# Attention decode on one Trainium2 core: moving the stationary block of the score matmuls 8b columns to the left

## Chip, cores, metric

One core of one Trainium2 chip. The metric is the device time of one execution in microseconds (us); less is better. Times are medians of several executions. Verdicts are "faster", "same" or "slower" with a threshold of 2%, or "unclear" when the interval holds the threshold. PE is the engine of the matmuls, PEld stands for its weight loads, DVE and ACT are the vector and the scalar engine, and SP is the engine whose queue issues the loads of the ring.

## The reference

A decoder block for one new token in each of four sequences: attention over the last 2048 cached keys, then a gated feed-forward layer. Cut to what matters:

```python
# B = 4 batches, D = 1024, Hq = 32 query heads, Hkv = 4 key heads, Dh = 128, W = 2048, F = 3584
q = (layernorm(x) @ wq).reshape(B, 1, Hq, Dh).transpose(0, 2, 1, 3)
k = repeat(k_cache[:, :, -W:, :], 8, axis=1)
v = repeat(v_cache[:, :, -W:, :], 8, axis=1)
p = softmax(einsum("bhqd,bhkd->bhqk", q, k) * Dh ** -0.5)
o = einsum("bhqk,bhkd->bhqd", p, v)
h = x + o.reshape(B, 1, Hq * Dh) @ wo
l = layernorm(h)
out = h + (silu(l @ w1) * (l @ w3)) @ w2
```

Each key head g serves eight query heads, and the four batches have separate softmaxes: 4 batches x 4 key heads x 8 queries are 128 rows of scores.

## The kernel before

Everything that comes from HBM goes through one ring of 160 KiB per partition. The loads are issued from one queue, in this order; a load is issued as soon as the last reader of the ring space that it overwrites is done.

```python
plan = [
    ("wq", load_rows, (0, wq_v, N_Q, 0, 4)),
    ("wq", load_rows, (32 * KIB, wq_v, N_Q, 4, 4)),
    ("k", load_kv, (64 * KIB, A_k_cache, 0)),      # keys of batches 0, 1
    ("k", load_kv, (96 * KIB, A_k_cache, 2)),      # keys of batches 2, 3
    ("v", load_kv, (128 * KIB, A_v_cache, 0)),     # values of batches 0, 1
    ("v", load_kv, (0, A_v_cache, 2)),             # values of batches 2, 3
    ("wo", load_rows, (32 * KIB, wo_v, D, 0, 32)),
    ("w1", load_rows, (96 * KIB, w1_v, N_F, 0, 8)),
    ("w3", load_rows, (0, w3_v, N_F, 0, 4)),
    # ... (w3's other half, w2 in four pieces)
]
```

w1 overwrites the keys of batches 2 and 3 and most of the values of batches 0 and 1. So it waits for the output matmuls of batches 0 and 1, which come after all scores and the softmax.

The queries are copied into a zeroed tile `qz`. Batch b has a region of 136 columns: for each key head g a block of 32, whose first 8 columns hold the queries, and 8 spare columns at the end.

```python
qz = act.tile([P, B, Hkv * QD + REP], BF16)        # QD = 32, REP = 8
nc.vector.memset(qz[:], 0.0)
# ... q matmuls, scaling, transposes
nc.vector.tensor_copy(
    out=qz[:, :, : Hkv * QD].rearrange("p b (g z) -> p b g z", g=Hkv)[:, :, :, :REP],
    in_=qt_ps[:].rearrange("p r (g x) -> p x g r", g=Hkv)[:, :B, :, :],
)
qz_v = qz[:].rearrange("p b y -> p (b y)")
# ...
def emit_scores(u):                                 # unit u: batch b, 512 keys n
    b, n = units[u]
    kT_v = kT_tiles[u][:].rearrange("d j (pp g) -> d g j pp", g=Hkv)
    for g in range(Hkv):
        z0 = (b * Hkv + g) * QD
        nc.tensor.matmul(
            scores_ps[QD * g : QD * (g + 1), n * 512 : (n + 1) * 512],
            lhsT=qz[:, b, g * QD : (g + 1) * QD],
            rhs=kT_v[:, g, :, :],
            start=(b == 0),
            stop=(b == B - 1),
        )

for u, (b, n) in enumerate(units):
    # ... 16 transposes of keys on PE, evicted to kT half by DVE, half by ScalarE
    if u >= 1:
        emit_scores(u - 1)
# ... row maximum, exponential over all 128 rows, transposes of the probabilities
for b in range(B):
    for j in range(JK):
        nc.tensor.matmul(OT_ps[:, b, :], lhsT=loaded["v"][b][:, j, :], ...)
    if b % BS == BS - 1:
        load_next()
```

In this kernel a column of a stationary block (128x32) becomes one of the 32 rows of scores that its matmul writes. In this version the queries of every batch stand in columns 0 to 7 of their block, so `start` and `stop` add the four batches' scores up in the same eight rows of each group, and the other 24 rows hold zeros.

## Time and profile before

| | before |
|---|---|
| time, median of 3 runs | 138.38 us (138.34 to 138.45) |
| profiled run | 138.12 us, span 136.3 us |
| bytes through the queue of the ring loads | 55.58 MB, 95.3% of sixteen engines' span |
| busy PE / DVE / ACT | 50% / 31% / 23% |
| score stage, start of first to start of last matmul | 29.6 to 54.9 us |
| w1 issued | 73.22 us |

The page of the kernel before: span, busy time of each engine, the granted TensorE clock in tenths over 40 slices, the DMA queue (packets, megabytes, share), and the chain that ended last, by engine and by line.

```profile
span 136.3 us, 2302 instructions
...
PE 67.9 (50%) x1035; PEld 42.9 (31%) x1035; DVE 42.6 (31%) x73; ACT 31.0 (23%) x36; POOL 1.7 (1%) x8
...
PEclk9999999999999999965555865897557777555577
...
q1 hardware_dynamic: 2592, 55.58, 95.3%
...
DMA 58%; PE 21%; ACT 13%; DVE 5%; issue 1%; SPq 0%; ACTq 0%
DMA ring<-in_B_w_dram 42%; DMA ring<-in_A_wq_dram 16%; PE kt_ps L263 9%; ACT kT L269 6%; PE scores_ps L248 5%; ACT z L304 3%; PE q_ps L215 2%; PE g_ps L403 2%; DVE rmax L280 2%; ACT Pm L285 2%; PE OT_ps L326 2%; DVE pT L294 1%; DVE z L300 1%; ACT L285 1%; DVE q_sb L225 1%
```

The DMA queue is busy 95.3% of the span, while no engine is busy much over half of it: the kernel is a stream of 55.58 MB with the arithmetic beside it. But the chain also lists PE, ACT and DVE with 39% together, and names the score matmuls with 5%. A chain lists what was last at each step.

The instructions of the query tile: count, shortest/median/longest in ns, first and last start in us.

```profile
L248 PEld LDWEIGHTS <-qz x64: 92/92/93, 29.4 to 54.9; 128*32 128x32 bf16 x64
L248 PE MATMUL scores_ps<-kT,qz x64: 608/609/612, 29.6 to 54.9; 128*32 128x512 bf16 x64
```

The 64 weight loads read blocks at four different offsets (272 bytes from batch to batch) and differ by 1 ns.

The PE timeline of the stretch before the scores (start us, us taken, what, and in brackets the idle time before it), and then the ring's queue around 73 us:

```profile
22.55 3.15 PE L215 MATMUL q_ps<-ring,xnT 128*4 128x512 bf16 x32 [5.92 <-DMA ring<-in_A_wq_dram]
...
27.45 2.03 PE L263 MATMUL kt_ps<-ident,ring 128*128 128x128 bf16 x33
29.62 0.62 PE L248 MATMUL scores_ps<-kT,qz 128*32 128x512 bf16 x4 [0.15 <-ACT kT L269]
```

```profile
73.22 0.33 SPq L93 DMA_DIRECT2D ring<-in_B_w_dram  x1
```

Stretches of the span. The last three columns are granted clock, mean share of the DMA engines, and GB/s.

```profile
core 0: us, PE busy (x) PEld busy (x) DVE busy (x) ACT busy (x) POOL busy (x), PEclk, DMA share, GB/s
15.00:30.00 15.00, 7.89 (x93) 3.82 (x85) 2.36 (x4) 2.04 (x3) 0.00 (x0) 1.00 0.97 416
30.00:45.00 15.00, 13.46 (x179) 9.17 (x175) 5.70 (x9) 8.39 (x9) 0.00 (x0) 1.00 1.01 428
45.00:57.00 12.00, 9.13 (x112) 5.47 (x109) 5.41 (x7) 5.97 (x6) 0.00 (x0) 1.00 1.00 427
76.00:84.00 8.00, 3.56 (x92) 2.97 (x96) 1.32 (x3) 0.00 (x0) 0.00 (x0) 0.71 0.94 403
84.00:90.00 6.00, 5.05 (x104) 3.92 (x96) 1.35 (x5) 0.00 (x0) 0.00 (x0) 0.79 0.98 423
```

From 15 to 57 us, where the scores are made, the DMA engines are at 0.97 to 1.01. They don't run short while PE works. (The view puts a packet's whole bytes and time down to the stretch in which it starts, which is how a share comes out over 1.)

### The profile page before, as it was taken

What the parts mean: (1) busy time and instruction counts of PE and PEld (TensorE: products, weight loads), DVE (VectorE), ACT (ScalarE), POOL (GpSimd) and SP (SyncE); (2) the same over time, 40 slices, a digit from 0 to 9 for tenths busy, and PEclk for the clock granted to TensorE, in tenths of its full rate; (3) what the DMA queues carried; (4) which work ended last, traced back from release to release, by engine and by line L of the source; (5) the groups of instructions that cost most, each with busy time, mean ns of one, the idle gap of its engine ahead of it and who ended that gap; (6) DMA issues with size and microseconds to landing.
All of it is one profiled execution on the core that took longest, in us unless ns stands there. A gap on an engine that the chain in (4) does not pass through costs nothing.

```text
span 136.3 us, 2302 instructions
## 1 busy us (share of the span) xinstructions
PE 67.9 (50%) x1035; PEld 42.9 (31%) x1035; DVE 42.6 (31%) x73; ACT 31.0 (23%) x36; POOL 1.7 (1%) x8
## 2 busy tenths in 40 slices
PE   0101803698989889105259538830096440900960
PEld 0100201274656565001149427610043210300840
DVE  6440000244444444609940030160000695070000
ACT  0400000155555646092944000000003300000001
POOL 5000000000000000000000000000000000000000
PEclk9999999999999999965555865897557777555577
DMA  5999899999999999997988989989799999989960
GB/s 156 462 462 443 385 413 418 423 447 423 428 437 409 437 437 423 435 582 341 538 385 365 524 365 442 459 353 522 328 412 463 434 437 447 429 388 409 426 261 5
DMA packets 2662, 55.75 MB, mean 409 GB/s; under 512 B 312, under 2 KB 344, under 8 KB 604
## 3 DMA queue, kind: packets, MB, share of 16 engines
q1 hardware_dynamic: 2592, 55.58, 95.3%
q8 instruction: 8, 0.13, 0.3%
q10 hardware_dynamic: 60, 0.02, 0.1%
q14 instruction: 2, 0.02, 0.0%
HBM read 55.59 MB, written 0.01 MB: 408 GB/s over the span
## 4 chain that ended last, share of the span: by engine, by line
DMA 58%; PE 21%; ACT 13%; DVE 5%; issue 1%; SPq 0%; ACTq 0%
DMA ring<-in_B_w_dram 42%; DMA ring<-in_A_wq_dram 16%; PE kt_ps L263 9%; ACT kT L269 6%; PE scores_ps L248 5%; ACT z L304 3%; PE q_ps L215 2%; PE g_ps L403 2%; DVE rmax L280 2%; ACT Pm L285 2%; PE OT_ps L326 2%; DVE pT L294 1%; DVE z L300 1%; ACT L285 1%; DVE q_sb L225 1%
## 5 line engine op out<-in xcount | busy, mean ns | idle before, releaser
L269 ACT COPY kT<-kt_ps 128x1024 bf16<-128x1024 bf16 x16 | 15.8, 1014 | 12.0 <-PE kt_ps L263 12.0
L263 PE MATMUL kt_ps<-ident,ring 128*128 128x128 bf16 x256 | 16.4, 219 | 0.0
L263 PEld LDWEIGHTS <-ring 128*128 128x128 bf16 x256 | 14.3, 98 | 5.0 <-issue 4.9
L267 DVE COPY kT<-kt_ps 128x1024 bf16<-128x1024 bf16 x16 | 11.1, 691 | 15.2 <-PE kt_ps L263 15.2
L215 PE MATMUL q_ps<-ring,xnT 128*4 128x512 bf16 x64 | 6.7, 596 | 12.0 <-DMA ring<-in_A_wq_dram 12.0
L403 PEld LDWEIGHTS <-hnT 128*32 128x32 bf16 x128 | 5.3, 137 | 23.1 <-issue 20.5
L248 PE MATMUL scores_ps<-kT,qz 128*32 128x512 bf16 x64 | 9.9, 609 | 3.1 <-ACT kT L269 3.1
L326 PE MATMUL OT_ps<-z,ring 128*128 128x32 bf16 x256 | 7.4, 185 | 6.7 <-ACT z L304 5.0
L403 PE MATMUL u_ps<-ring,hnT 128*32 128x448 bf16 x64 | 6.3, 572 | 8.3 <-DMA ring<-in_B_w_dram 8.3
L403 PE MATMUL g_ps<-ring,hnT 128*32 128x448 bf16 x64 | 5.4, 525 | 9.0 <-DMA ring<-in_B_w_dram 9.0
L433 PE MATMUL y_ps<-ring,hgT 128*32 128x256 bf16 x112 | 5.7, 370 | 8.4 <-DMA ring<-in_B_w_dram 8.3
L326 PEld LDWEIGHTS <-ring 128*128 128x128 bf16 x256 | 7.3, 103 | 7.4 <-issue 7.4
L433 PEld LDWEIGHTS <-hgT 128*32 128x32 bf16 x112 | 4.4, 129 | 10.3 <-issue 6.1
L215 PEld LDWEIGHTS <-xnT 128*4 128x4 bf16 x64 | 2.1, 116 | 16.2 <-issue 15.9
L353 PE MATMUL y_ps<-ring,o 128*32 128x256 bf16 x128 | 5.8, 365 | 2.0 <-DMA ring<-in_A_wo_dram 2.0
L443 ACT CAST res<-y_ps 128x256 bf16<-128x256 f32 x1 | 0.4, 372 | 26.5 <-PE y_ps L433 26.5
L304 ACT ACTIVATE z<-pt_ps,mask 128x512 bf16<-128x512 f32 x8 | 5.3, 687 | 3.5 <-DVE z L300 3.5
L225 DVE TENSOR_SCALAR q_sb<-q_ps 128x512 bf16<-128x512 f32 x1 | 0.7, 690 | 17.2 <-PE q_ps L215 17.2
L353 PEld LDWEIGHTS <-o 128*32 128x32 bf16 x128 | 4.8, 130 | 3.8 <-issue 3.1
L300 DVE TENSOR_SCALAR z<-pt_ps,mask 128x512 bf16<-128x512 f32 x8 | 5.5, 740 | 1.2 <-ACT z L304 0.8
L296 PE MATMUL pt_ps<-pT,perm 128*128 128x512 bf16 x4 | 2.4, 607 | 6.8 <-DVE pT L294 6.8
L417 DVE RECIPROCAL eg<-eg 128x896 f32<-128x896 f32 x1 | 5.8, 5753 | 0.0
(73 smaller groups left out, 40.5 us busy)
## 6 DMA issues: line engine op xcount, KB each, us to landing
ring<-in_A_wq_dram SPq DMA_DIRECT2D x2, 4096.0 KB, 16.8
ring<-in_A_k_cache_dram SPq DMA_DIRECT2D x4, 2048.0 KB, 25.5
ring<-in_A_v_cache_dram SPq DMA_DIRECT2D x4, 2048.0 KB, 40.2
ring<-in_B_w_dram SPq DMA_DIRECT2D x1, 7168.0 KB
ring<-in_B_w_dram SPq DMA_DIRECT2D x2, 3584.0 KB, 28.6
ring<-in_B_w_dram SPq DMA_DIRECT2D x1, 4352.0 KB
ring<-in_B_w_dram SPq DMA_DIRECT2D x1, 1792.0 KB
ring<-in_B_w_dram SPq DMA_DIRECT2D x1, 768.0 KB
```

The source lines that it names most:

```text
L215: nc.tensor.matmul(q_ps[QD * g : QD * g + B, hf * 512 : (hf + 1) * 512], lhsT=xnT[:, kc, :], rhs=wq_t[:, c0 : c0 + 512], start=(kc == 0), ...
L248: nc.tensor.matmul(scores_ps[QD * g : QD * (g + 1), n * 512 : (n + 1) * 512], lhsT=qz[:, b, g * QD : (g + 1) * QD], rhs=kT_v[:, g, :, :], ...
L263: nc.tensor.transpose(out=kt_ps[:, jj, :], in_=k_v[:, n * NJ + t * TB + jj, :], identity=ident[:])
L267: nc.vector.tensor_copy(out=kT[:, t * TB : (t + 1) * TB, :], in_=kt_ps[:])
L269: nc.scalar.copy(out=kT[:, t * TB : (t + 1) * TB, :], in_=kt_ps[:])
L300: nc.vector.tensor_scalar(out=z[:, :, g, :], in0=pt_ps[:], scalar1=mask[:, g : g + 1], scalar2=None, op0=ALU.mult)
L304: nc.scalar.mul(out=z[:, :, g, :], in_=pt_ps[:], mul=mask[:, g : g + 1])
L326: nc.tensor.matmul(OT_ps[:, b, :], lhsT=loaded["v"][b][:, j, :], rhs=PTz[j // NJ][:, (j % NJ) * B + b, :, :], start=(j == 0), stop=(j == J ...
L353: nc.tensor.matmul(y_ps[QD * j : QD * (j + 1), :], lhsT=o4[:, i, :, :].rearrange("p b s -> p (b s)"), rhs=loaded["wo"][i][:, j * CG : (j + ...
L403: nc.tensor.matmul(out_ps[QD * j : QD * (j + 1), hf, :HF], lhsT=hnT[:, k, :], rhs=loaded[kind][k][:, c0 : c0 + HF], start=(k == 0), stop=( ...
L417: nc.vector.reciprocal(out=eg[:], in_=eg[:])
L433: nc.tensor.matmul(y2_ps[QD * j : QD * (j + 1), :], lhsT=hgT[:, i, :], rhs=loaded["w2"][i][:, j * CG : (j + 1) * CG], start=False, stop=(i ...
```

## The change

The tile has the 8 spare columns so that a window of 32 columns can slide: started 8b columns further left, it holds batch b's queries in its columns 8b to 8b+7 and zeros elsewhere. The four batches then accumulate into rows of their own.

```diff
             nc.tensor.matmul(
                 scores_ps[QD * g : QD * (g + 1), n * 512 : (n + 1) * 512],
-                lhsT=qz[:, b, g * QD : (g + 1) * QD],
+                lhsT=qz_v[:, z0 : z0 + QD],
                 rhs=kT_v[:, g, :, :],
```

(b * 136 + 32g - 8b is b * 128 + 32g, which is z0.) The compiled instruction streams of the two kernels list the same operations, shapes and waits on all engines. One operand address differs.

Both versions pass the comparison with the reference, though only the later one computes it. A float32 calculation with the reference's formulas explains this: the scores have a standard deviation of 0.0025, so every softmax is nearly uniform. With batch 0's scores replaced by the sum over the batches and those of batches 1 to 3 by zero, as the earlier kernel's rows have it, the output moves by at most 8e-7, with a standard deviation of 0.05 of the output. These inputs can't tell right scores from wrong ones.

## The prediction

> **What bounds the kernel now.** HBM traffic. The page's DMA queue table gives 55.58 MB through the weight-and-cache queue at 95.3% of the sixteen engines' span. PE, DVE and ACT are busy 50%, 31% and 23%. The chain of waits is 58% DMA. PE (21%) and ACT (13%) enter it mostly from 27 to 55 us, where it alternates between key transposes, the ScalarE copy of kT (1.02 us) and four score matmuls (0.62 us). DMA is not short of work there: its share from 15 to 57 us is 0.97 to 1.01 (stretch table). The next load that this stage can hold back, w1, is issued at 73.2 us, when the second batch's output matmuls have freed its ring space; the previous load, wo, is still in flight then. Estimate: the loads up to wo are 33.6 MB, at about 428 GB/s (stretch table) 78 us, plus the 2 us start, so they end near 80 us. The score stage therefore has an estimated 5 to 7 us of slack.
>
> **What the change does.** It alters one operand address. The stationary block of the 64 score matmuls (16 units x 4 groups) has 128 x 32 bf16 in both versions, and only its first column moves, by 8b. Rows of scores: before, batch b's eight queries occupy columns 0 to 7 of each 32-column block for every b, and start/stop accumulate all four batches into the same rows. After, they are columns 8b to 8b+7; the other 24 are zeros of the same tile. So this repairs the meaning (four separate softmaxes); nothing is removed or added. The comparison of compiled instruction streams shows all five engines the same, 2063 PE rows in both, with the same waits.
>
> **Costs, from the trace.** 64 weight loads of 92 ns (min 92, max 93; 2.4 us) and 64 matmuls of 609 ns (608 to 612), four groups overlapping in 0.62 us. [...] Alignment: before, the blocks start at multiples of 272 bytes per batch, after at multiples of 256, yet before's 64 loads, over four different offsets, already differ by 1 ns at most. Net on this stage: 0.0 us, at most 0.1. Downstream, max (2.29 us), exponential (1.97 us) and the rest keep their shapes; only values change.
>
> [...] The granted clock before is 1.00 throughout the score stage and 0.50 to 0.73 later, where PE idles often.
>
> **On the critical path:** nothing. Even 5% of all score matmuls (0.5 us of 9.9) would disappear in the slack.
>
> **Prediction:** 138.4 us, range 137.9 to 138.9 (before: 138.34 to 138.45, its profiled run 138.12). Faster by over 2%: 1%; within 2%: 98%; slower by over 2%: 1%.
>
> **Signs that it is right:** 64 score weight loads of 92 ns and matmuls of 609 ns; last score matmul near 55 us; w1 issued near 73 us; 95% DMA share; PE clock 1.0 until 57 us. **Signs that it is wrong:** score weight loads over 100 ns, or w1 issued after 80 us with a dip in the DMA row behind it.
>
> **What would make it wrong:** a different chip or HBM state; a weight load that is dearer when its block straddles two batches' regions; an operand-dependent clock drop in the softmax or output stage large enough to push w1's issue past wo's end.

The sum came to 138.4 us, the time before plus 0.0 us (at most 0.1) for the change, with 5 to 7 us of slack (about 80 us for the end of wo, less 73.2 us for w1's issue). That the addresses would cost nothing was the estimate from the 1 ns by which the 64 loads of the trace differ; that the values would cost nothing was not shown by the trace. e4 and e3 test them. The 2 us start is read from the trace (the first packets of wq start at 1.74 us). PE was busy 88% of the score stage and 44% of the time from 57 to 136 us; the clocks of 0.50 to 0.73 are means of stretches of 8 to 16 us there.

## The result

| | before | after |
|---|---|---|
| time, median | 138.36 us (138.17 to 138.45, 4 runs) | 138.22 us (138.14 to 138.38, 4 runs) |
| ratio | | 0.9996, 95% interval 0.9981 to 1.0011 |
| score stage, first to last matmul | 29.6 to 54.9 us | 31.6 to 56.9 us |
| w1 issued | 73.22 us | 75.27 us |

Ratios are the mean time of one kernel's runs over that of the other's of the same rounds, so not quite the ratio of the medians quoted.

The page of the kernel after, the same lines:

```profile
span 136.5 us, 2302 instructions
...
PE 69.7 (51%) x1035; PEld 44.0 (32%) x1035; DVE 42.6 (31%) x73; ACT 31.1 (23%) x36; POOL 1.7 (1%) x8
...
PEclk9999999999999999965555555896558655555586
...
q1 hardware_dynamic: 2592, 55.58, 95.1%
...
DMA 56%; PE 24%; ACT 11%; DVE 5%; issue 1%; SPq 0%; ACTq 0%
DMA ring<-in_B_w_dram 40%; DMA ring<-in_A_wq_dram 16%; PE kt_ps L263 11%; ACT kT L269 5%; PE scores_ps L248 5%; ACT z L304 3%; PE q_ps L215 3%; PE g_ps L403 2%; DVE rmax L280 2%; ACT Pm L285 2%; PE OT_ps L326 1%; DVE pT L294 1%; DVE z L300 1%; ACT L285 1%; PE qt_ps L229 1%
```

The instructions of the query tile in the kernel after:

```profile
L248 PEld LDWEIGHTS <-qz x64: 92/92/102, 31.6 to 56.9; 128*32 128x32 bf16 x64
L248 PE MATMUL scores_ps<-kT,qz x64: 608/609/630, 31.6 to 56.9; 128*32 128x512 bf16 x64
```

Medians of 92 and 609 ns, as before; the longest are a little longer. The stage takes the same 25.3 us from first to last start. Yet it begins 2.0 us later, and w1 is issued 2.05 us later. The PE timeline and the ring's queue of the kernel after show from where on:

```profile
22.57 3.58 PE L215 MATMUL q_ps<-ring,xnT 128*4 128x512 bf16 x32 [6.10 <-DMA ring<-in_A_wq_dram]
...
27.98 3.73 PE L263 MATMUL kt_ps<-ident,ring 128*128 128x128 bf16 x33
31.64 0.64 PE L248 MATMUL scores_ps<-kT,qz 128*32 128x512 bf16 x4
```

```profile
75.27 0.33 SPq L93 DMA_DIRECT2D ring<-in_B_w_dram  x1
```

The second batch of q matmuls took 3.58 us where it had taken 3.15, and the first 33 key transposes 3.73 us where they had taken 2.03. Both precede the first score matmul, so the changed operand had not been used once. The later transposes take 1.07 us for 16 in both traces. It isn't later data either: PE's wait for wq ended at 22.55 and 22.57 us. And the stretches of the kernel after:

```profile
core 0: us, PE busy (x) PEld busy (x) DVE busy (x) ACT busy (x) POOL busy (x), PEclk, DMA share, GB/s
15.00:30.00 15.00, 8.08 (x75) 4.08 (x68) 1.68 (x3) 0.66 (x2) 0.00 (x0) 1.00 0.97 416
30.00:45.00 15.00, 13.65 (x172) 9.41 (x170) 5.54 (x8) 8.34 (x9) 0.00 (x0) 1.00 1.01 428
45.00:57.00 12.00, 10.42 (x136) 6.74 (x133) 4.84 (x7) 7.50 (x8) 0.00 (x0) 1.00 1.01 429
76.00:84.00 8.00, 4.79 (x153) 4.12 (x153) 1.33 (x3) 0.00 (x0) 0.00 (x0) 0.50 0.92 395
84.00:90.00 6.00, 5.11 (x118) 3.75 (x110) 1.34 (x5) 0.00 (x0) 0.00 (x0) 0.80 1.03 442
```

The DMA share is as before, and the total doesn't show the 2 us. The trace shows where they fade: the matmuls with wo start at 82.25 us before and 83.16 us after, because before they waited 2.04 us for wo to land, and after only 0.81 us for the eviction ahead of them. The first gate matmul starts at 99.06 us before and 98.96 us after, in both when w1 has landed.

So two things were left to show: that the lag has nothing to do with the change, and how much lag the stream of loads really absorbs. The latest issue of w1 that costs nothing is called the knee below; from the prediction's estimate of wo's end I first put it at 79.7 us.

### The profile page after: what moved, and what is told of

The parts are those of the page before. It is cut to its first block, busy times and chain, and to the rows that moved or that the text cites. A ratio compares the mean times of both kernels' runs of the same rounds, so it can differ in the third digit from the quotient of the medians.

```text
span 136.5 us, 2302 instructions
## 1 busy us (share of the span) xinstructions
PE 69.7 (51%) x1035; PEld 44.0 (32%) x1035; DVE 42.6 (31%) x73; ACT 31.1 (23%) x36; POOL 1.7 (1%) x8
## 3 DMA queue, kind: packets, MB, share of 16 engines
q1 hardware_dynamic: 2592, 55.58, 95.1%
## 4 chain that ended last, share of the span: by engine, by line
DMA 56%; PE 24%; ACT 11%; DVE 5%; issue 1%; SPq 0%; ACTq 0%
DMA ring<-in_B_w_dram 40%; DMA ring<-in_A_wq_dram 16%; PE kt_ps L263 11%; ACT kT L269 5%; PE scores_ps L248 5%; ACT z L304 3%; PE q_ps L215 3%; PE g_ps L403 2%; DVE rmax L280 2%; ACT Pm L285 2%; PE OT_ps L326 1%; DVE pT L294 1%; DVE z L300 1%; ACT L285 1%; PE qt_ps L229 1%
## 5 line engine op out<-in xcount | busy, mean ns | idle before, releaser
L263 PE MATMUL kt_ps<-ident,ring 128*128 128x128 bf16 x256 | 18.1, 232 | 0.0
L263 PEld LDWEIGHTS <-ring 128*128 128x128 bf16 x256 | 16.0, 105 | 4.9 <-issue 4.9
L215 PE MATMUL q_ps<-ring,xnT 128*4 128x512 bf16 x64 | 7.2, 626 | 12.0 <-DMA ring<-in_A_wq_dram 12.0
L326 PEld LDWEIGHTS <-ring 128*128 128x128 bf16 x256 | 7.4, 105 | 7.4 <-issue 7.4
L353 PE MATMUL y_ps<-ring,o 128*32 128x256 bf16 x128 | 5.2, 343 | 0.8 <-DVE o L342 0.8
L226 ACT ACTIVATE q_sb<-q_ps 128x512 bf16<-128x512 f32 x1 | 0.6, 597 | 21.4 <-DVE q_sb L225 21.4
```

The lines of the kernel that those rows point to most:

```text
L215: nc.tensor.matmul(q_ps[QD * g : QD * g + B, hf * 512 : (hf + 1) * 512], lhsT=xnT[:, kc, :], rhs=wq_t[:, c0 : c0 + 512], start=(kc == 0), ...
L263: nc.tensor.transpose(out=kt_ps[:, jj, :], in_=k_v[:, n * NJ + t * TB + jj, :], identity=ident[:])
L353: nc.tensor.matmul(y_ps[QD * j : QD * (j + 1), :], lhsT=o4[:, i, :, :].rearrange("p b s -> p (b s)"), rhs=loaded["wo"][i][:, j * CG : (j + ...
```

## The experiments

My theory: the changed address costs nothing at all. The 2.0 us belong to the execution and not to the change. (What I took for their cause was a guess that no run shows; it is cut from the expectations of e1 and e12.) They, and any other lag of the score stage, vanish as long as w1 is issued before the load ahead of it runs out. Rivals: the lag comes from the change; the data in the block change the clock; a weight load pays for its start address; the score stage is on the critical path, as the chain lists it, and something else made up for it.

### e1: the kernel before, once more

No edit.

> The kernel before, unedited, timed against itself: it measures the noise and gives a second trace of the same program. My theory (the 2.0 us by which the kernel after reached its first score matmul later, 31.6 against 29.6 us, is [...] not the change): ratio 1.000 with an interval of about 0.2%; the first score matmul anywhere from 29.5 to 31.7 us, a late one would settle it. Rival (the lag comes from the change): 29.6 us within 0.2 us, as in the first trace of before.

138.16 us (138.12 to 138.28, 5 runs), ratio 0.9996 (0.9984 to 1.0009). The PE timeline of this run:

```profile
22.62 3.58 PE L215 MATMUL q_ps<-ring,xnT 128*4 128x512 bf16 x32 [5.92 <-DMA ring<-in_A_wq_dram]
...
28.03 3.73 PE L263 MATMUL kt_ps<-ident,ring 128*128 128x128 bf16 x33
31.69 0.64 PE L248 MATMUL scores_ps<-kT,qz 128*32 128x512 bf16 x4
```

The unchanged kernel started its scores at 31.7 us here, with the same 3.58 and 3.73 us ahead of it, and issued w1 at 75.31 us. The rival is refuted: the lag belongs to the execution, not to the change.

### e2: the kernel after, once more

No edit.

> The kernel after, unedited, five rounds. My theory: ratio to before 0.998 to 1.002; score weight loads 92 ns and score matmuls 609 ns in the median; the first score matmul anywhere from 29.5 to 31.7 us. Rival (the lag comes from the change): first score matmul again at 31.6 us within 0.2 us. Rival (the shifted operand costs something): ratio above 1.002.

138.17 us (137.96 to 138.23, 5 runs), ratio 0.9994 (0.9981 to 1.0006); medians 92 and 609 ns (93 and 609 in e1); first score matmul at 31.6 us. The last number alone is what the rival expected as well; only e1, e3 and e4 tell them apart. The kernel before timed against itself (0.9996) and the kernel after (0.9994) can't be distinguished.

### e3: non-zero data in the idle columns

```diff
-    nc.vector.memset(qz[:], 0.0)
+    nc.vector.memset(qz[:], 0.05)
```

> After, with the query tile filled with 0.05 in place of 0.0 before the queries are copied in, so the 24 idle columns of each stationary block hold non-zero data (the scores are wrong on purpose). My theory: nothing depends on the values; ratio 0.998 to 1.002, weight loads 92 ns, matmuls 609 ns, granted clock 1.00 up to 57 us. Rival (operand data move the clock): a granted clock below 1.00 in the score stage, or matmuls over 620 ns in the median, and the stage from first to last score matmul longer than the 25.3 us of both first traces by over 1 us.

138.15 us (138.10 to 138.33, 4 runs), ratio 0.9997 (0.9983 to 1.0011); granted clock 1.00 from 30 to 57 us, where the stage lies. The query tile's instructions in this run:

```profile
L248 PEld LDWEIGHTS <-qz x64: 92/92/93, 29.8 to 55.3; 128*32 128x32 bf16 x64
L248 PE MATMUL scores_ps<-kT,qz x64: 608/609/611, 30.0 to 55.3; 128*32 128x512 bf16 x64
```

25.3 us from first to last start again. Neither the time nor the durations depend on these data. And with the changed address of the kernel after, the first score came at 30.0 us: an early start isn't tied to the kernel before either.

### e4: blocks that start at odd places

```diff
-                lhsT=qz_v[:, z0 : z0 + QD],
+                lhsT=qz_v[:, z0 + 3 : z0 + 3 + QD],
```

> After, with every stationary block starting three columns (6 bytes) further right, so that no block starts at a multiple of 16 bytes and blocks straddle neighbouring regions (scores are wrong on purpose). My theory: start address is free; weight loads 92 ns, matmuls 609 ns, ratio 0.998 to 1.002. Rival (a weight load pays for its start address): weight loads above 95 ns in the median; if by 10%, 9 ns times 64 is 0.6 us of load time, hidden in the total.

138.34 us (138.05 to 138.44, 4 runs), ratio 1.0001 (0.9984 to 1.0018). The query tile's instructions in this run:

```profile
L248 PEld LDWEIGHTS <-qz x64: 92/93/95, 29.5 to 55.0; 128*32 128x32 bf16 x64
L248 PE MATMUL scores_ps<-kT,qz x64: 608/609/612, 29.7 to 55.0; 128*32 128x512 bf16 x64
```

One ns more in the median than in before; but e1, the kernel before unedited, has 93 ns too. The start address is free within what this trace resolves. (First score at 29.7 us.)

### e5, e6, e7: a longer score stage

After each group of four score matmuls of a unit, the same four with an all-zero stationary block, X times; the result stays correct.

```diff
+    zz = act.tile([P, QD], BF16)
+    nc.vector.memset(zz[:], 0.0)
 ...
-        for g in range(Hkv):
+        X = 1 if b < 2 else 0              # e5;  e6: X = 1;  e7: X = 2
+        for rep in range(1 + X):
+            for g in range(Hkv):
 ...
-                lhsT=qz_v[:, z0 : z0 + QD],
+                lhsT=qz_v[:, z0 : z0 + QD] if rep == 0 else zz[:],
-                start=(b == 0),
-                stop=(b == B - 1),
+                start=(b == 0 and rep == 0),
+                stop=(b == B - 1 and rep == X),
```

> After, with each score matmul of batches 0 and 1 followed by one of the same shape with an all-zero stationary block (32 more matmuls, correct result). Estimate: 8 units times 0.55 to 0.62 us, some of it in PE's waits for ScalarE, so the stage grows by 3 to 5 us. My theory (slack: time is 138.3 plus whatever w1's issue exceeds about 79.7 us, the estimate for when the load before it runs out): w1 issued at 76 to 80 us, time 138.2 to 139.0. Rival (the stage is on the critical path, as the chain of waits lists it): 141.2 to 143.3.

138.22 us (138.12 to 138.48, 4 runs), ratio 1.0013 (0.9996 to 1.0029). The stage grew less than expected, to 26.6 us (30.0 to 56.6; in before a group of four took 0.62 us, and what followed it started 0.55 us after it), and w1 was issued at 74.95 us, which is no later than in e1. So this run is too weak to test much: it shows only that 32 more matmuls cost nothing that can be told from the noise.

> The same for all batches, 64 more matmuls (correct result): stage longer by 7 to 10 us. My theory: w1 issued at 80.5 to 85 us, time 139 to 143.5, that is 138.3 plus (w1's issue minus 79.7) within 1 us, with a dip in the DMA row before 85 us. Rival (critical path): 145 to 148.

139.31 us (139.07 to 139.72, 4 runs), ratio 1.0091 (1.0072 to 1.0109), clear of the noise. The stage runs from 30.1 us to the last start at 60.0, longer by 4.6 us, not by 7 to 10; w1 was issued at 78.30 us, earlier than I expected, and the time still rose by 1.2 us. So the knee lies well before 79.7 us. The dip expected in the DMA row isn't there: the share from 78 to 80 us is 0.56, and 0.46 in e2, which lost nothing. Had the stage been critical from its first us, as the rival has it, the 4.6 us would have shown as about 142.7 us.

> Two extra zero matmuls after each score matmul, 128 more (correct result): stage longer by 16 to 20 us. My theory: w1 issued at 89 to 95 us, the DMA row near zero for several us before it, time 147.5 to 153.5, that is 138.3 plus (w1's issue minus 79.7) within 1 us. The slope between this run and the one with 64 more is then one us of time per us of stage. Rival (critical path from the first us): 154 to 158.

145.32 us (145.31 to 146.45, 4 runs), ratio 1.0543 (1.0506 to 1.0581). The stage is longer by 11.4 us (30.0 to 66.7), the time by 7.2 us; both missed their ranges from below. The ring's queue and the stretches of this run:

```profile
85.07 0.33 SPq L93 DMA_DIRECT2D ring<-in_B_w_dram  x1
```

```profile
core 0: us, PE busy (x) PEld busy (x) DVE busy (x) ACT busy (x) POOL busy (x), PEclk, DMA share, GB/s
78.00:80.00 2.00, 0.69 (x17) 0.58 (x16) 1.96 (x5) 1.91 (x3) 0.00 (x0) 0.50 0.38 164
80.00:82.00 2.00, 1.94 (x35) 1.51 (x35) 0.92 (x2) 0.88 (x2) 0.00 (x0) 0.50 0.00 0
82.00:84.00 2.00, 0.40 (x15) 0.40 (x15) 0.75 (x1) 1.16 (x3) 0.00 (x0) 0.50 0.00 0
84.00:86.00 2.00, 2.00 (x82) 2.00 (x78) 0.00 (x0) 0.85 (x1) 0.00 (x0) 0.50 0.04 8
```

This is the hole that was looked for: DMA share 0.00 from 80 to 84 us, because every packet that had been issued had started before and w1's load was issued only at 85.07. Its edges, in stretches of 0.2 us (a packet counts whole where it starts, so that such short shares go over 1):

```profile
79.00:79.20 0.20, 0.00 (x0) 0.00 (x0) 0.20 (x2) 0.20 (x1) 0.00 (x0) 0.50 2.27 983
79.20:79.40 0.20, 0.10 (x4) 0.09 (x4) 0.20 (x1) 0.20 (x2) 0.00 (x0) 0.50 0.00 0
85.80:86.00 0.20, 0.20 (x14) 0.20 (x11) 0.00 (x0) 0.00 (x0) 0.00 (x0) 0.50 0.00 0
86.00:86.20 0.20, 0.20 (x15) 0.20 (x11) 0.00 (x0) 0.00 (x0) 0.00 (x0) 0.50 6.04 2007
```

The last packets of wo start before 79.2 us, the first of w1 at 86.0 or a little later, about 0.9 us after the issue. By the packet records in the trace file a packet of 64 KiB takes 2.4 us in the median, and wo's last one ends at 81.6 us. From start to start the hole is 6.8 us long, the loss 7.2. By the sum with 79.7 us the time should have been 143.7 us; the 1.6 us more say again that I had put the knee too late. From e6 to e7 w1's issue moved by 6.8 us and the median time by 6.0. All three predictions of the stage's growth were too high: some of the extra matmuls ran in PE's waits for the evictions. The score matmuls waited for ScalarE's copies of kT for 3.1 us in eight waits in before, and for 0.2 us in one in e7.

### e8: three quarters of the score matmuls left out

```diff
+        if b > 0:
+            return
         for g in range(Hkv):
 ...
-                stop=(b == B - 1),
+                stop=True,
```

> After, with the score matmuls of batches 1 to 3 left out (48 of 64 gone; batches 1 to 3 get uniform attention, wrong on purpose). Transposes and copies of the keys stay. My theory: w1 issued 4 to 9 us earlier, time 138.0 to 138.5, ratio within 0.3%: even most of the score work is worth nothing. Rival (critical path): 4 to 9 us faster. Correctness: I expect it to pass, since the scores have a standard deviation of 0.0025 by a calculation with the reference, so the softmax is nearly uniform whatever the rows.

138.49 us (138.22 to 138.64, 4 runs), ratio 1.0026 (1.0011 to 1.0041). w1 was issued at 58.34 us, 15 us earlier than in the first trace of before, more than I expected: with the scores of batches 1 to 3 gone, the softmax no longer waits for their key transposes (the row maximum starts at 34.7 us in place of 55.6). None of the 15 us reached the total. Why it is even 0.26% slower I didn't find out. The result passed as correct, with uniform attention for three of the four batches: a measured sign that the comparison can't see the scores.

### e9: w1 later, score stage untouched

```diff
-    for b in range(B):
+    for b in (2, 3, 0, 1):
         for j in range(JK):
 ...
-        if b % BS == BS - 1:
-            load_next()
+        if b == 1:
+            load_next(2)
```

> After, with the score stage untouched and the output matmuls done for batches 2, 3, 0, 1 instead of 0, 1, 2, 3, so that the ring space of w1 comes free at the end of that stage (correct result). From the two runs with longer score stages the knee is re-estimated at 77.5 us: time is 138.2 plus (w1's issue minus 77.5). My theory (w1's issue is the only way by which this part of the kernel reaches the total): issue at 78.5 to 81.5 us, time 139.0 to 142.5 and within 0.8 us of that sum. Rival (longer score stages cost time for another reason, for example the later w3 and w2 loads or PE): 138.0 to 138.6, as PE does the same work in the same time.

140.99 us (140.37 to 141.62, 4 runs), ratio 1.0207 (1.0173 to 1.0241): slower, though whether by over 2% is unclear. The score matmuls of the profiled run, at 140.37 us, and the ring's queue (seven loads merged; the first is w1's):

```profile
L248 PE MATMUL scores_ps<-kT,qz x64: 608/609/611, 31.0 to 56.3; 128*32 128x512 bf16 x64
80.52 23.46 SPq L93 DMA_DIRECT2D ring<-in_B_w_dram  x7
```

w1 was issued at 80.52 us. The sum gives 138.2 + 3.0 = 141.2 us: 0.2 over the median, and 0.85 over that one run, just outside the 0.8 expected. Not one matmul was added, the score stage took its 25.3 us, and the kernel became about 2% slower when w1's issue moved. That is the mechanism without the score stage.

### e10, e11: w1 in two loads

```diff
-        ("w1", load_rows, (96 * KIB, w1_v, N_F, 0, 8)),
+        ("w1", load_rows, (96 * KIB, w1_v, N_F, 0, 4)),
+        ("w1", load_rows, (124 * KIB, w1_v, N_F, 4, 4)),
 ...
+    load_next()
     emit_scores(len(units) - 1)
```

e10 is this in e7, e11 is this in the kernel after.

> The kernel with 128 extra score matmuls (145.3 us), with the load of w1 split in two: its first four rows go to the ring space of the last two batches' keys, which is free when their transposes are done, and only the other four wait for the first two batches' values. Estimate: the first half is 3.67 MB, 8.6 us at 428 GB/s, so the knee for the second half moves from 77.5 to about 86 us, and it is issued near 85. My theory: 138.0 to 139.5 us, although the PE work stays. Rival (the added PE work itself costs): 144 to 146.

139.75 us (139.58 to 140.02, 4 runs), ratio 1.0118 (1.0103 to 1.0133). With the same 128 extra matmuls, and scores that end as late (66.6 us), 5.6 of e7's 7.2 us are gone. The first half of w1 was issued at 62.00 us and the second at 84.97, and the DMA share from 76 to 84 us is 0.89 in place of 0.40. It missed my upper bound by 0.25 us: 1.6 us over before remain, which this doesn't explain. From 84 to 120 us the DMA share is 0.99 to 1.01, so they aren't one hole behind the score stage. The trace shows where most of them fall: PE's wait for the second half of w3 ends at 116.07 us in this run and at 115.98 in before, but its last wait for w2 ends at 133.68 in place of 132.38. Why the end drags wasn't found out.

> After, with the same split load of w1 and no extra matmuls: more slack where none is needed. My theory: first half issued near 55 to 58 us, ratio 0.998 to 1.002. Rival (the stage before still costs something): faster by over 0.3%.

138.22 us (138.15 to 138.30, 4 runs), ratio 1.0008 (0.9991 to 1.0024), with the first half issued at 54.10 us. More slack is worth nothing where there is enough.

### e12: extra matmuls ahead of the scores, with a mistake

Twenty matmuls were to keep PE busy while it waits for the second half of wq.

```diff
         if kc == RQ - 1:
             load_next()
+            warm_ps = psA.tile([P, 512], FP32, tag="kt2")
+            for _ in range(20):
+                nc.tensor.matmul(warm_ps[:], lhsT=ident[:], rhs=wq_t[:, :512], start=True, stop=True)
```

> After, with 20 matmuls of 128x512 into an unused PSUM tile in the wait for the second half of wq (correct result). My theory [...]: the second batch of q matmuls takes under 2.5 us instead of 3.2 to 3.6, every key transpose has 219 ns and none 300, the first score matmul starts at 27.5 to 29.4 us, earlier than in every trace so far, and the time stays at 0.998 to 1.002. Rival (the lag is something else, such as data arrival): first score matmul at 29.6 us or later.

170.24 us (169.80 to 170.49, 4 runs), ratio 1.232 (1.2299 to 1.2342), result correct. Who waited for whom (total us, times, longest):

```profile
PE warm_ps L226 <- DMA ring<-in_A_v_cache_dram: 30.0, 1, 30.0
```

I had put the matmuls behind the call that loads the values of batches 2 and 3 into the same ring space. In program order they read those values, not wq, and so PE stood 30 us for them in the middle of the transposes. The run says nothing about its question; whether keeping PE busy there would remove the lag stays open (what the lag follows is read from the traces below). By accident it is the longest lag of all, and it checks the rule: w1 was issued at 110.34 us, and 138.2 + (110.34 - 77.5) is 171.0, against 170.24 measured. (wo was late here as well, issued at 78.52 us; the sum only asks for the last load held back.)

### All runs side by side

The time from w1's issue to the end is the profiled run's time less the issue; it includes about 1.8 us outside the span, which all runs have.

| run | first and last score matmul, us | w1 issued, us | time of the profiled run, us | issue to end, us |
|---|---|---|---|---|
| before | 29.6, 54.9 | 73.22 | 138.12 | 64.9 |
| after | 31.6, 56.9 | 75.27 | 138.27 | 63.0 |
| e1 before again | 31.7, 57.0 | 75.31 | 138.18 | 62.9 |
| e2 after again | 31.6, 56.9 | 75.25 | 138.18 | 62.9 |
| e3 dense data | 30.0, 55.3 | 73.65 | 138.16 | 64.5 |
| e4 odd start | 29.7, 55.0 | 73.30 | 138.44 | 65.1 |
| e5 32 extra | 30.0, 56.6 | 74.95 | 138.21 | 63.3 |
| e8 48 fewer | 29.8, 34.0 | 58.34 | 138.62 | 80.3 |
| e6 64 extra | 30.1, 60.0 | 78.30 | 139.37 | 61.1 |
| e9 w1 later | 31.0, 56.3 | 80.52 | 140.37 | 59.9 |
| e7 128 extra | 30.0, 66.7 | 85.07 | 145.33 | 60.3 |
| e12 PE held 30 us | 31.0, 92.0 | 110.34 | 170.49 | 60.2 |

Two regimes. In the upper eight rows the total is 138.1 to 138.6 us, whether w1 is issued at 58 or 75 us: the stream of loads decides. In the lower four the end follows w1's issue by 59.9 to 61.1 us, while w1's issue itself moves by 32 us. The lower four average 60.3 us, so the lines cross at about 138.2 - 60.3 = 77.9 us (77.1 by e6 alone, 78.3 by e9). How sharp the bend is stays open: no run issued w1 between 75.3 us, which cost nothing, and 78.3, which cost 1.2.

The hole before w1 isn't always the whole loss. PE's wait for the second half of w3 ends at 115.98 us in before, and 1.3 us later in e6, 2.35 in e9 and 7.2 in e7. The spans are longer by 1.3, 2.3 and 7.2 us. So in these three the loss is complete when w3 has landed. In e10, where that wait ends only 0.1 us late and the last one for w2 1.3, most of it arises in the loads of w2, and that part isn't explained.

The trace files also show what the lag of the first score goes with. They hold records of the granted clock, each with its start. The last record of full clock that begins before 32 us, and the first score matmul of the same trace:

| run | before | e4 | e8 | e10 | e3 | e5 | e6 | e7 | e9 | e12 | e11 | after | e2 | e1 |
|---|---|---|---|---|---|---|---|---|---|---|---|---|---|---|
| full clock from, us | 25.13 | 25.28 | 25.50 | 25.62 | 26.05 | 26.24 | 26.50 | 26.55 | 30.28 | 30.38 | 31.36 | 31.80 | 31.83 | 31.84 |
| first score, us | 29.6 | 29.7 | 29.8 | 29.9 | 30.0 | 30.0 | 30.1 | 30.0 | 31.0 | 31.0 | 31.5 | 31.6 | 31.6 | 31.7 |

The later the clock rises, the later the scores start, to within 0.1 us; in after, e2 and e1 it rises only once the first score matmuls have begun. Where it rises among the transposes (e9, e12, e11), these take 311 to 314 ns before, and the first with 250 ns or less starts within 0.1 us of the record. So the lag goes with the clock and not with the operand. The kernel before stands at both ends of the table. Why the clock rises at another moment each time, no run here tested.

## Why the prediction was right

The time, 138.22 us, is within 0.2 us of the predicted 138.4, and "within 2%" had 98%. Point by point:

- **What bounds the kernel.** Right: 95.3% DMA share before, 95.1% after, and e8 and e11 show that less work or more slack in front of w1 brings nothing.
- **The change costs 0.0 us in the score stage.** Right: the same instructions, medians of 92 or 93 and 609 ns, 25.3 us from first to last matmul, in before, after, e1, e2, e3 and e4 alike. The two doubts named, operand data and straddling blocks, were tested by e3 and e4 and found empty. The granted clock of e3 was 1.00 from 30 to 57 us.
- **Nothing of it on the critical path, "5 to 7 us of slack".** The mechanism was right, the size a little too large. From w1's issue at 73.22 us in the first trace to the knee at about 77.9 us are 4.7 us; in an execution with a late start of the scores (75.3 us) only 2.6. The mis-sized term is the end of wo "near 80 us", taken as the latest issue of w1. wo's last packet ends at 81.6 to 81.8 us by the packet records of before, after and e7 (so the first matmuls with wo waited until 82.25 in before), but what must not run out are the packets still to start. In e7 the last of wo started before 79.2 us, and from there the 0.9 us between a load's issue and its first packets have to be taken off, which my sum didn't name: 79.2 - 0.9 = 78.3 us, close to the knee.
- **The signs.** "Last score matmul near 55 us" and "w1 issued near 73 us" failed in the trace of after (56.9 and 75.27 us), though the kernel was unharmed. I took one trace's instants for properties of the kernel. e1 shows the unchanged kernel doing the same. Durations of single instructions and lengths of stages (92 ns, 609 ns, 25.3 us) were the sound signs.
- **"PE clock 1.0 until 57 us"** came true and was worth little: that row reads full speed up to 57 us in both traces, even where the same 33 transposes took 3.73 us in one and 2.03 us in the other. It counts the time before the first clock record as full speed, and that record begins at 25.13 us in before and at 31.80 in after.

No version that ran beats both kernels. The gain of the change is that it computes the reference's rows.

## What to carry to other kernels

When only an operand's address changes and the compiled streams list the same instructions, shapes and waits, expect the same time (here 138.22 us after 138.36), and check it by durations of instructions and lengths of stages rather than by instants. When a stage is listed on the chain of waits of a kernel that is bound by its loads, ask which later load's issue it holds back and how long the load ahead of it lasts: here a lag was free up to an issue at 75.3 us at least, and beyond the knee of about 77.9 us it cost about one us per us (6.0 us of time for 6.8 us of issue from e6 to e7). And see whether the inputs can tell a wrong result from a right one at all; here leaving out three quarters of the score matmuls passed.

## What else these traces show

- The moment of full clock varies from execution to execution: PE's second batch of q matmuls starts at 22.5 to 22.7 us, the record of full clock between 25.1 and 31.8, and the first score matmul between 29.6 and 31.7, in the unchanged kernel too (29.6 and 31.7). Such a lag moves the issue of a load by the same 2 us (73.2 to 75.3) and so takes almost half of the 4.7 us of slack. What sets the moment was not shown; the run meant to test a guess about it failed.
- The clock records held here: in e9, e12 and e11 the first transpose of 250 ns or less, after ones of 311 to 314, starts within 0.1 us of the record of full clock. What misled was the row on the profile's page, which shows 1.00 where no record has come yet (in after up to 31.80 us, with transposes of 314 ns).
- The key transposes ran at two rates: 33 in a row take 2.03 us in before (62 ns each), after the record of full clock and before any score matmul, against 3.73 us in after (113 ns each), before the record.
- A weight load of a 32-column score block has 92 ns in the median, one of a 128-column key block in the same stretch 98 ns. Why they differ by so little was not tested.
- In e7 the first packets of w1 are recorded about 0.9 us after its issue begins (85.07 to 86.0), with the queue empty. The issuing instruction itself takes 0.33 us, and from its end it is about 0.6 us.
- The loads moved 428 GB/s from 30 to 45 us in both traces, with one core running.
